# Attention and a gated FFN in one kernel: weights and first q/k by casting DMA, a new order of the first rows, masks as products on VectorE, FFN tiles of 368 and 208 tokens

## The chip, the cores and the metric

The kernel runs on one core of a Trainium2 chip. The time is the device time of one execution in microseconds (us), and the executions of one kernel spread by 0.6 to 2.2% in these runs (the four of the kernel before: 441.25 to 444.32 us). Each profile is of one execution. Its span is about 2 us shorter than the time reported for the run. TensorE (PE in the profile) does the matmuls, VectorE is DVE, ScalarE is ACT, GpSimd is POOL, and SyncE (SP) issues most DMAs. The granted clock is the share of the full clock that TensorE got, as the profile shows it. Results of matmuls stand in PSUM buffers, of which the program has a fixed number, until DVE or ACT has read them. Numbers like L330 are lines of the kernel that was profiled, so the same statement has different numbers in different kernels.

## The reference, cut to what matters

```python
def _attn_ref(q, k, v, beacon_k, beacon_v):     # q, k, v: (8, 8, 576, 64) f32, beacon: 16 keys
    k_all = np.concatenate([beacon_k, k], axis=2)
    v_all = np.concatenate([beacon_v, v], axis=2)
    scores = scale * np.matmul(q, k_all.transpose(0, 1, 3, 2))
    causal[:, Nb:] = np.triu(np.ones((S, S), dtype=bool), k=1)   # beacons are always visible
    scores = np.where(causal, -1000000000.0, scores)
    ...                                          # softmax
    return np.matmul(a, v_all)

def _moe_ref(x, w_gate, w_val, w_out):           # x: (4608, 512), d_ff = 1536
    gate = np.maximum(x @ w_gate, 0.0)
    val = x @ w_val
    return gate * val @ w_out                    # out: (4608, 512) f32

# x is the attention output with the 8 heads of a token side by side
```

There are 8 batches of 576 tokens. All matmuls run on bf16 operands, and all inputs are f32 in HBM, so every input must be cast on its way.

## The kernel before

Attention is done in 64 "bursts": one for each batch, pair of heads, and group of query rows. Group 0 is the first 368 rows, group 1 the last 208. A burst has two score tiles. ACT takes the exponentials of both, POOL zeroes the masked part of the result in place, TensorE multiplies by v (the AV matmuls), and DVE divides by the sum. When the four pairs of a batch are done, its rows of x are turned into xT and the FFN can use them.

```python
    def softmax(u, i):
        segs, cols = SLABS[u.g][i]
        p = psb.tile([P, 2, 512], BF16, name="p")
        A.activation(p[:, :, :cols], u.s[i][:, :, :cols], AF.Exp, scale=scale)
        for (kt, q0, n, c, mask) in segs:
            if mask:
                c, m, base = mask
                G.affine_select(out=p[:, :, c:c + m], in_=p[:, :, c:c + m], ...)   # POOL
        u.p.append(p)
```

Every load goes in f32 through one ring of 14 staging tiles, issued by SP, and is then cast by DVE, ACT or POOL (`cast(G)`). The output stores go through SP's queue too. `pump` refills the ring in one fixed order:

```python
        todo = (pq[0, 0] + [bk[0]] + pq[0, 1] + vl[0] + pq[0, 2] + pq[0, 3] + ch[0]
                + [bk[1]] + pq[1, 0] + ch[1] + pq[1, 1] + vl[1] + ch[2] + pq[1, 2] + pq[1, 3] + wol)
        def pump():
            while todo and Load.open < NSTG:
                todo.pop(0).issue()          # pq: q and k of a pair, vl: v, ch and wol: weights
```

In batches 0 and 1 the bursts go pair by pair, both row groups of a pair in turn, so that all 8 bursts of batch 0 are over before any FFN work. The FFN runs on nine tiles of 512 tokens, each with 12 pairs of gate and value matmuls (`up`) and 4 groups of output matmuls (`down`). A budget spreads it over the later bursts; one of these with its FFN work is a "tick":

```python
        def up(nf):                                       # 12 of these per tile
                for ki in range(KM): nc.tensor.matmul(g, wg[...], xT[:, ki, m0:m0 + 512], ...)
                A.activation(gs, g, AF.Relu)
                for ki in range(KM): nc.tensor.matmul(u, wv[...], xT[:, ki, m0:m0 + 512], ...)
                V.tensor_mul(st["h"][:, nf, :], gs, u)
        def down(ms):                                     # 4 of these per tile
                ...                                       # 12 matmuls of 512 columns
                A.copy(ob, o)
                nc.sync.dma_start(out[...], ob)
```

Of the kernel before, what the change touches and what calls it, by code (L numbers as in the profile page):

```python
# [22 lines left out]
def general_path(tc, q, k, v, beacon_k, beacon_v, out, ident, wg, wv, wo):  # L23
# [79 lines left out]
    with tc.tile_pool(name="gen_sb2", bufs=1) as sb, \  # L103
# [29 lines left out]
    ((((0, 0, 368, 0, (0, 112, 16)), (2, 240, 128, 368, (368, 128, 0))), 496),  # L133
     (((1, 112, 256, 0, (0, 128, 0)),), 256)),
    ((((0, 368, 208, 0, None), (1, 368, 208, 208, None), (4, 496, 80, 416, (416, 80, 0))), 496),
     (((2, 368, 208, 0, None), (3, 368, 208, 208, (208, 128, 0))), 416)),
# [6 lines left out]
def kernel(  # L143
# [24 lines left out]
    M_TILE = 512  # L168
    R = 2 * S // P
    scale = 1.0 / (D ** 0.5)  # L170
    assert (Nb, S, D, H) == (16, 576, 64, 8)

    const = ctx.enter_context(tc.tile_pool(name="const", bufs=1))
    ident = const.tile([P, P], BF16, name="ident")
    make_identity(nc, ident)
    ones = const.tile([P, 1], BF16, name="ones")
    nc.vector.memset(ones, 1.0)
# [5 lines left out]
    nc.vector.memset(rall, 1.0)  # L183
# [3 lines left out]
    qTs, kTs, vs = [], [], []  # L187
    for i in range(2):
        qTs.append(ring.tile([P, NP, S], BF16, name=f"qT{i}"))
        kT = ring.tile([P, NP, NKT * P], BF16, name=f"kT{i}")  # L190
        nc.gpsimd.memset(kT[:, :, Stot:], 0.0)
        kTs.append(kT)
        vx = ring.tile([P, NKT, H, D + 2], BF16, name=f"vx{i}")
        nc.gpsimd.memset(vx[:, :, :, D:], 1.0)
        vs.append(vx)

    NSTG = 14
    stage = main.enter_context(tc.tile_pool(name="stage", bufs=NSTG))
    c16 = main.enter_context(tc.tile_pool(name="c16", bufs=8))
# [3 lines left out]
    osb_p = main.enter_context(tc.tile_pool(name="osb", bufs=2))  # L203
# [3 lines left out]

    V, G, A = nc.vector, nc.gpsimd, nc.scalar
# [4 lines left out]
    class Load:  # L213
# [7 lines left out]
        def issue(self):  # L221
            Load.open += 1
            self.st = st = stage.tile([P, 576], FP32, name="stg")
            dma = nc.sync.dma_start
            heads = st[:, :H * D].rearrange("p (h d) -> p h d", d=D)
            if self.kind == "pair":
                src, b, p = self.key
                dma(st, src[b, 2 * p:2 * p + 2].rearrange("h (p r) d -> (h p) (r d)", r=R))
            elif self.kind == "beacon_k":
                dma(heads[:Nb], rows_of(beacon_k, self.key[0], 0, Nb))  # L230
            elif self.kind == "w":
                dst, src, ko, n0 = self.key
                dma(st[:, :512], src[ko * P:(ko + 1) * P, n0:n0 + 512])
            else:
                src, beacon, b, t = self.key
                s0 = t * P
                if beacon is not None:
                    s0 -= Nb
                self.n = n = min(P, S - s0)
                if s0 < 0:  # L240
                    dma(heads[:Nb], rows_of(beacon, b, 0, Nb))
                    dma(heads[Nb:], rows_of(src, b, 0, P - Nb))
                    self.n = P
                else:
                    dma(heads[:n], rows_of(src, b, s0, s0 + n))
            return self

        def cast(self, eng):
            Load.open -= 1
            cp = eng.copy if eng is A else eng.tensor_copy  # L250
            if self.kind == "w":
                dst, src, ko, n0 = self.key
                cp(dst[:, ko, n0:n0 + 512], self.st[:, :512])
            elif self.kind == "v":
                b, t, n = self.key[2], self.key[3], self.n
                cp(vs[b % 2][:n, t, :, 0:D], self.st[:n, :H * D].rearrange("p (h d) -> p h d", d=D))  # L256
            else:
                self.c = c = c16.tile([P, 576], BF16, name="c16")
                n, w = {"pair": (P, 576), "beacon_k": (Nb, 512)}.get(self.kind) or (self.n, 512)
                cp(c[:n, :w], self.st[:n, :w])  # L260
            return self

        def turn(self, cp):

            c = self.c
            if self.kind == "pair":
                src, b, p = self.key
                tp = f_ps.tile([P, R, D], BF16, name="f")
                for r in range(R):
                    for a in range(2):  # L270
                        rows = slice(a * D, (a + 1) * D)
                        nc.tensor.transpose(tp[rows, r], c[rows, r * D:(r + 1) * D], ident[rows, rows])  # L272
                dst = kTs[b % 2][:, p, Nb:Stot] if src is k else qTs[b % 2][:, p, :]
                cp(dst.rearrange("q (p r) -> q p r", r=R), tp.rearrange("q r p -> q p r"))  # L274
            elif self.kind == "beacon_k":
                tp = f_ps.tile([P, NP, Nb], BF16, name="f")
                for p in range(NP):
                    nc.tensor.transpose(tp[:, p], c[:Nb, p * P:(p + 1) * P], ident[:Nb, :Nb])
                cp(kTs[self.key[0] % 2][:, :, 0:Nb], tp)
            else:  # L280
                b, t, n = self.key[2], self.key[3], self.n
                dst = (kTs if self.kind == "k" else qTs)[b % 2]
                nc.sync.dma_start_transpose(dst[:, :, t * P:t * P + n], c[:n, :d_model])


# [3 lines left out]
    def qk(u):  # L289
        u.s, u.p = [], []  # L290
        for segs, cols in SLABS[u.g]:
            s = s_ps.tile([P, 2, 512], FP32, name="s")
            for (kt, q0, n, c, _) in segs:
                for a in range(2):
                    rows = slice(a * D, (a + 1) * D)
                    nc.tensor.matmul(s[:, a, c:c + n], kTs[u.b % 2][rows, u.pi, kt * P:(kt + 1) * P],  # L296
                                     qTs[u.b % 2][rows, u.pi, q0:q0 + n], start=True, stop=True)
            u.s.append(s)

    def softmax(u, i):  # L300
        segs, cols = SLABS[u.g][i]
        p = psb.tile([P, 2, 512], BF16, name="p")
        A.activation(p[:, :, :cols], u.s[i][:, :, :cols], AF.Exp, scale=scale)  # L303
        for (kt, q0, n, c, mask) in segs:
            if mask:
                c, m, base = mask
                G.affine_select(out=p[:, :, c:c + m], in_=p[:, :, c:c + m],  # L307
                                pattern=[[0, 2], [1, m]], compare_op=ALU.is_ge, fill=0.0,
                                base=base, channel_multiplier=-1)
        u.p.append(p)  # L310

    def av(u, opool):
# [3 lines left out]
        for p, (segs, cols) in zip(u.p, SLABS[u.g]):  # L316
            for (kt, q0, n, c, _) in segs:
                for j, qi in enumerate(qt):
                    r0, rn = QROWS[qi]
                    if q0 <= r0 and r0 + rn <= q0 + n:  # L320
                        blocks[j, kt] = (p, c + r0 - q0)
        first = True
        for j, qi in enumerate(qt):
            kts = sorted(kt for (jj, kt) in blocks if jj == j)
            m = 80 if qi == 4 else P
            for a in range(2):
                for kt in kts:
                    p, c = blocks[j, kt]
                    kr = P if kt < 4 else KT4
                    nc.tensor.matmul(o[:m, j, a, 0:D + 1], p[:kr, a, c:c + m],  # L330
                                     vs[u.b % 2][:kr, kt, 2 * u.pi + a, 0:D + 1],
                                     start=first, stop=(kt == kts[-1]), skip_group_check=True)
# [9 lines left out]
        if u.last:  # L342
            for qi in qt:
                r0, rn = QROWS[qi]
                dst = xT[:, :, u.b * S + r0:u.b * S + r0 + rn]
                if u.b:
                    nc.sync.dma_start_transpose(dst, u.x[:rn, qi, :])
                    continue
                tp = f_ps.tile([P, KM, P], BF16, name="f")
                for ki in range(KM):  # L350
                    nc.tensor.transpose(tp[:, ki, :rn], u.x[:rn, qi, ki * P:(ki + 1) * P], ident[:rn, :rn])
                (V.tensor_copy if qi % 2 else A.copy)(dst, tp[:, :, :rn])


    def ffn_tile(m):
        m0 = m * M_TILE
        st = {}

        def up(nf):
            def go():  # L360
                if nf == 0:
                    st["h"] = fsb.tile([P, NF, M_TILE], BF16, name="hT")
                g = f_ps.tile([P, M_TILE], FP32, name="f")
                for ki in range(KM):
                    nc.tensor.matmul(g, wg[:, ki, nf * P:(nf + 1) * P], xT[:, ki, m0:m0 + M_TILE],  # L365
                                     start=(ki == 0), stop=(ki == KM - 1))
                gs = fsb.tile([P, M_TILE], FP32, name="g")
                A.activation(gs, g, AF.Relu)  # L368
                u = f_ps.tile([P, M_TILE], FP32, name="f")
                for ki in range(KM):  # L370
                    nc.tensor.matmul(u, wv[:, ki, nf * P:(nf + 1) * P], xT[:, ki, m0:m0 + M_TILE],  # L371
                                     start=(ki == 0), stop=(ki == KM - 1))
# [235 lines left out]
```

## Time and profile before

| | before |
|---|---|
| time, median of 3 runs | 443.14 us (442.43 to 444.32) |
| span of the profile, mean granted clock | 438.5 us, 0.964 |
| TensorE busy | 377.0 us (86%) |
| DVE, ACT, POOL busy | 150.3, 193.2, 134.6 us |
| first FFN matmul | 36.0 us |

The next lines are from the page of the kernel before: busy time of each engine, then the span in 40 equal slices of 11 us (each digit is the busy share in tenths; PEclk is the granted TensorE clock), then the main DMA queue with its packets, its MB and its share of the 16 DMA engines' span.

```profile
span 438.5 us, 8104 instructions
PE 377.0 (86%) x3085; PEld 187.2 (43%) x3085; DVE 150.3 (34%) x349; ACT 193.2 (44%) x282; POOL 134.6 (31%) x295
...
PE   3668658784649979999999899999989989999995
...
PEclk9989988996859999999999999999999999999999
DMA  9954894798995278973984697559872012002002
...
q1 hardware_dynamic: 155936, 59.04, 62.4%
```

TensorE is nearly full from the thirteenth slice on (one slice shows 7). Before that it is partly idle throughout, with a hole in slices 10 to 12 (99 to 132 us) where the digits are 4, 6 and 4, while the DMA engines are at 8, 9 and 9 tenths and the clock falls to 6, 8 and 5. The table by windows of the kernel before measures the same in stretches. The columns are the window, its length, and for each engine its busy us and number of instructions (PE, weight loads, DVE, ACT, POOL), then the granted clock, the DMA share and GB/s.

```profile
0.00:24.00 24.00, 11.80 (x210) 8.55 (x210) 9.76 (x22) 10.44 (x13) 10.38 (x31) 1.00 1.00 273
24.00:60.00 36.00, 25.83 (x326) 15.20 (x326) 19.54 (x48) 16.32 (x24) 16.75 (x34) 0.95 0.67 204
60.00:90.00 30.00, 22.96 (x260) 12.39 (x261) 16.13 (x36) 12.76 (x18) 15.73 (x30) 0.89 0.74 182
90.00:135.00 45.00, 26.39 (x126) 10.49 (x125) 4.95 (x9) 9.57 (x16) 14.35 (x27) 0.77 0.98 181
135.00:170.00 35.00, 30.96 (x282) 15.60 (x281) 10.53 (x30) 18.20 (x26) 10.74 (x26) 1.00 0.48 109
```

From 90 to 135 us only 126 matmuls were issued, at a mean clock of 0.77. The waits of TensorE in the kernel before (who waited for whom, us in total, how often, longest) name the releasers:

```profile
PE f L272 <- DVE c L260: 16.4, 7, 4.7
PE o L330 <- POOL p L307: 13.7, 7, 9.8
PE s L296 <- ACT p L303: 9.6, 12, 1.2
PE f L365 <- ACT ob L383: 4.8, 1, 4.8
```

The first line, q and k that wait for their casts on DVE before TensorE can transpose them, is the longest in total, but all of it lies before 90 us. Two lines belong to the hole: AV (L330) waits for a POOL mask (L307), and an FFN group (L365) waits for the output copy on ACT (L383). To see why the mask was late, read POOL's own timeline in the kernel before (start us, duration, instruction, in brackets the idle time before it and what ended it):

```profile
117.86 0.61 POOL L256 CAST vx<-stg 128x512 bf16<-128x512 f32 x1 [4.33 <-DMA stg<-in_v_dram]
...
123.26 0.61 POOL L256 CAST vx<-stg 128x512 bf16<-128x512 f32 x1 [2.83 <-DMA stg<-in_v_dram]
124.44 0.61 POOL L260 CAST c<-stg 128x512 bf16<-128x512 f32 x1 [0.57 <-DMA stg<-in_k_dram]
125.52 0.61 POOL L260 CAST c<-stg 128x512 bf16<-128x512 f32 x1 [0.46 <-DMA stg<-in_q_dram]
126.08 1.10 POOL L307 TENSOR_SCALAR_AFFINE_SELECT p<-p 128x224 bf16<-128x224 bf16 x3
```

POOL took its instructions in the order of its program: the exponentials that ACT did before this mask had ended at 117.75 us, but the mask started at 126.08. It took 0.4 us a piece, and it stood behind casts that each waited for a load. TensorE's timeline shows the price in its first line (9.76 us), and the wait for the copy in its second:

```profile
108.03 1.87 PE L365 MATMUL f<-xT,wg 128*128 128x512 bf16 x4 [4.82 <-ACT ob L383]
...
126.52 0.35 PE L330 MATMUL o<-vx,p 128*128 128x65 bf16 x3 [9.76 <-POOL p L307]
```

The copy itself waited for its buffer, which a store in SP's queue had to free; that is ACT's timeline of the kernel before:

```profile
100.84 0.58 ACT L383 COPY ob<-f 128x512 f32<-128x512 f32 x1 [8.18 <-DMA out_dram<-ob]
107.40 0.58 ACT L383 COPY ob<-f 128x512 f32<-128x512 f32 x1 [5.97 <-DMA out_dram<-ob]
```

SP issued loads and transposes almost without a pause from 81 to 135 us, and the stores stood among them: the copy that ended at 90.06 us had its store issued at 98.33.

### The profile page before, as it was taken

How to read it: one execution, taken by the hardware profiler on the slowest of the kernel's cores; microseconds unless marked ns; L12 is line 12 of the kernel's file. 1: busy time of each engine (PE TensorE's matmuls, PEld its weight loads, DVE VectorE, ACT ScalarE, POOL GpSimd, SP SyncE). 2: the span in 40 equal slices, each digit the busy share in tenths (PEclk: the TensorE clock that was granted, in tenths of full speed). 3: DMA queues.
4: the chain of work that ended last, by engine and by line, in shares of the span. 5: the costliest groups of instructions: out<-in, count | busy, mean ns of one | idle time of the engine just before them, and what ended most of it. 6: DMA issues, size and time to landing. Idle time of an engine off the chain costs nothing. (4 is left out here: it accounts for less than half of the span.)

```text
span 438.5 us, 8104 instructions
## 1 busy us (share of the span) xinstructions
PE 377.0 (86%) x3085; PEld 187.2 (43%) x3085; DVE 150.3 (34%) x349; ACT 193.2 (44%) x282; POOL 134.6 (31%) x295
## 2 busy tenths in 40 slices
PE   3668658784649979999999899999989989999995
PEld 2454333431214434454444444454444445544442
DVE  3454564600114313441342144134314422430520
ACT  3453535411316545554554456455545554423321
POOL 3453442822345115333332243334323211000000
PEclk9989988996859999999999999999999999999999
DMA  9954894798995278973984697559872012002002
GB/s 201 334 186 130 234 358 126 151 168 175 199 192 99 40 164 178 148 139 97 209 147 103 158 191 128 139 144 180 142 170 51 0 48 85 19 3 96 0 16 87
DMA packets 155981, 59.62 MB, mean 136 GB/s; under 512 B 144672, under 2 KB 144672, under 8 KB 155936
## 3 DMA queue, kind: packets, MB, share of 16 engines
q1 hardware_dynamic: 155936, 59.04, 62.4%
q8 instruction: 26, 0.43, 0.4%
q14 instruction: 19, 0.16, 0.1%
HBM read 38.27 MB, written 9.44 MB: 109 GB/s over the span
## 5 line engine op out<-in xcount | busy, mean ns | idle before, releaser
L373 DVE TENSOR_TENSOR hT<-g,f 128x512 bf16<-128x512 f32 x108 | 74.3, 688 | 153.3 <-PE f L371 128.1
L307 POOL TENSOR_SCALAR_AFFINE_SELECT p<-p 128x256 bf16<-128x256 bf16 (+2 forms) x160 | 60.4, 390 | 207.8 <-ACT p L303 203.0
L303 ACT ACTIVATE p<-s 128x992 bf16<-128x992 f32 (+2 forms) x128 | 108.3, 864 | 35.5 <-PE s L296 33.5
L365 PE MATMUL f<-xT,wg 128*128 128x512 bf16 x432 | 114.8, 389 | 7.6 <-ACT ob L383 4.8
L371 PE MATMUL f<-xT,wv 128*128 128x512 bf16 x432 | 113.8, 387 | 0.2 <-ACT ob L383 0.2
L368 ACT ACTIVATE g<-f 128x512 f32<-128x512 f32 x108 | 64.5, 597 | 93.2 <-PE f L365 92.2
L380 PE MATMUL f<-wo,hT 128*128 128x512 bf16 x432 | 96.9, 379 | 0.0
L371 PEld LDWEIGHTS <-wv 128*128 128x128 bf16 x432 | 43.0, 100 | 53.8 <-issue 4.8
L365 PEld LDWEIGHTS <-wg 128*128 128x128 bf16 x432 | 40.2, 100 | 51.4 <-issue 11.6
L383 ACT COPY ob<-f 128x512 f32<-128x512 f32 x36 | 21.1, 585 | 92.8 <-PE f L380 54.5
L380 PEld LDWEIGHTS <-hT 128*128 128x128 bf16 x432 | 41.2, 98 | 47.1
L330 PE MATMUL o<-vx,p 128*128 128x65 bf16 (+2 forms) x888 | 43.8, 200 | 14.2 <-POOL p L307 13.7
L330 PEld LDWEIGHTS <-p 128*128 128x128 bf16 (+2 forms) x960 | 38.9, 109 | 27.4 <-POOL p L307 15.3
L338 DVE RECIPROCAL rall<-o 128x2 f32<-128x2 f32 (+2 forms) x88 | 15.4, 175 | 98.2 <-PE o L330 96.4
L296 PE MATMUL s<-qT,kT 64*128 64x208 bf16 (+4 forms) x512 | 39.0, 265 | 11.0 <-ACT p L303 9.6
L260 POOL CAST c<-stg 128x512 bf16<-128x512 f32 (+2 forms) x67 | 40.9, 622 | 8.5 <-DMA stg<-in_k_dram 4.9
L296 PEld LDWEIGHTS <-kT 64*128 64x128 bf16 x512 | 19.8, 98 | 38.6 <-issue 34.1
L339 DVE TENSOR_TENSOR x<-o,rall 128x128 bf16<-128x128 f32 (+2 forms) x88 | 34.0, 387 | 3.2
L256 POOL CAST vx<-stg 128x512 bf16<-128x512 f32 (+1 forms) x40 | 24.4, 616 | 25.0 <-DMA stg<-in_v_dram 25.0
L272 PE MATMUL f<-ident,c 64*64 64x64 bf16 x288 | 8.7, 220 | 20.6 <-DVE c L260 16.4
L272 PEld LDWEIGHTS <-c 64*64 64x64 bf16 x288 | 7.2, 132 | 23.5 <-DVE c L260 18.8
L274 ACT COPY qT<-f 128x576 bf16<-128x576 bf16 x5 | 3.2, 638 | 14.0 <-PE f L272 14.0
(35 smaller groups left out, 56.6 us busy)
## 6 DMA issues: line engine op xcount, KB each, us to landing
out_dram<-ob SPq DMA_DIRECT2D x36, 256.0 KB, 2.2
stg<-in_v_dram SPq DMA_DIRECT2D x24, 256.0 KB, 4.2
stg<-in_q_dram SPq DMA_DIRECT2D x24, 256.0 KB, 3.9
stg<-in_k_dram SPq DMA_DIRECT2D x18, 256.0 KB, 4.1
stg<-in_moe_w_gate_dram SPq DMA_DIRECT2D x12, 256.0 KB, 4.9
stg<-in_moe_w_val_dram SPq DMA_DIRECT2D x12, 256.0 KB, 5.0
stg<-in_moe_w_out_dram SPq DMA_DIRECT2D x12, 256.0 KB, 5.5
stg<-in_k_dram SPq DMA_DIRECT2D x8, 288.0 KB, 5.7
```

The source lines that it names most:

```text
L256: cp(vs[b % 2][:n, t, :, 0:D], self.st[:n, :H * D].rearrange("p (h d) -> p h d", d=D))
L260: cp(c[:n, :w], self.st[:n, :w])
L296: nc.tensor.matmul(s[:, a, c:c + n], kTs[u.b % 2][rows, u.pi, kt * P:(kt + 1) * P], qTs[u.b % 2][rows, u.pi, q0:q0 + n], start=True, stop= ...
L303: A.activation(p[:, :, :cols], u.s[i][:, :, :cols], AF.Exp, scale=scale)
L307: G.affine_select(out=p[:, :, c:c + m], in_=p[:, :, c:c + m], pattern=[[0, 2], [1, m]], compare_op=ALU.is_ge, fill=0.0, base=base, channel ...
L330: nc.tensor.matmul(o[:m, j, a, 0:D + 1], p[:kr, a, c:c + m], vs[u.b % 2][:kr, kt, 2 * u.pi + a, 0:D + 1], start=first, stop=(kt == kts[-1] ...
L339: V.tensor_mul(u.x[:m, i0:i0 + j1 - j0, u.pi * P:(u.pi + 1) * P].rearrange("p j (a d) -> p j a d", a=2), o[:m, j0:j1, :, 0:D], r.unsqueeze ...
L365: nc.tensor.matmul(g, wg[:, ki, nf * P:(nf + 1) * P], xT[:, ki, m0:m0 + M_TILE], start=(ki == 0), stop=(ki == KM - 1))
L368: A.activation(gs, g, AF.Relu)
L371: nc.tensor.matmul(u, wv[:, ki, nf * P:(nf + 1) * P], xT[:, ki, m0:m0 + M_TILE], start=(ki == 0), stop=(ki == KM - 1))
L373: V.tensor_mul(st["h"][:, nf, :], gs, u)
L380: nc.tensor.matmul(o, st["h"][:, nf, ms * P:(ms + 1) * P], wo[:, nf, :], start=(nf == 0), stop=(nf == NF - 1))
```

## The change

The intent is to fill TensorE earlier. (1) The weights, and q and k of batches 0 and 1 except for one pair's first rows, are loaded by GpSimd's DMAs, which write bf16 directly; their staging and casts fall away, and they are issued in the order in which they are used. (2) The mask becomes a product with a constant triangle on DVE; POOL keeps the casts of later batches. (3) In all batches the first 368 rows of all four pairs come first, so that the FFN can start after 4 bursts. (4) FFN tiles have 368 and 208 tokens, the row groups of a batch, instead of 512. (5) The order in DVE's, ACT's and TensorE's programs changes with it, and the output gets 3 buffers instead of 2. The diff, cut to its core (lines left out are marked by dots, and the comments are added here):

```diff
-    M_TILE = 512
+    tri = const.tile([P, 2, 240], BF16, name="tri")        # ones at and above the diagonal
-    NSTG = 14
+    NSTG = 6
-    osb_p = main.enter_context(tc.tile_pool(name="osb", bufs=2))
+    osb_p = main.enter_context(tc.tile_pool(name="osb", bufs=3))
...
-        for (kt, q0, n, c, mask) in segs:
-            if mask:
-                c, m, base = mask
-                G.affine_select(out=p[:, :, c:c + m], in_=p[:, :, c:c + m], ...)
+    def mask(u):
+        for i, (segs, cols, m) in enumerate(SLABS[u.g]):
+            p = u.p[i]
+            V.tensor_mul(p[:, :, :m], p[:, :, :m], tri[:, :, :m])
...
+    tiles = []
+    for b in range(B):
+        tiles += [(b * S, 368), (b * S + 368, 208)]
...
-            order = ([(p, g) for p in range(NP) for g in range(2)] if b < 2
-                     else [(p, g) for g in range(2) for p in range(NP)])
-            for p, g in order:
+            for p, g in [(p, g) for g in range(2) for p in range(NP)]:
...
+        def wload(dst, src, n0, n1):
+            G.dma_start(dst[:, :, n0:n1], src[:, n0:n1].rearrange("(j p) n -> p j n", p=P))
...
+        vl[0][0].issue()
+        vl[0][1].issue()
+        ...
+        direct(c0, 0, 1, 2, 0)              # casting DMAs: k, q of pair 1, first 368 rows
+        ...
+        direct(c0, 0, 2, NP, 0)             # pairs 2 and 3
+        vl[0][0].cast(G)
+        for n0, n1 in ((0, 256), (256, 512)):
+            wload(wg, moe_w_gate, n0, n1)
+            wload(wv, moe_w_val, n0, n1)
+        ...
+        direct(c0, 0, 0, NP, 1)             # the last 208 rows of all pairs
+        for n0, n1 in ((512, 1024), (1024, 1536)):
+            wload(wg, moe_w_gate, n0, n1)
+            wload(wv, moe_w_val, n0, n1)
...
+        burst(bursts[3])
+        ...
+        x_turn(bursts[3])                   # rows 0 to 367 of xT, by TensorE
+        next_ffn()
+        next_ffn()
+        ...
+        for p in range(NP):
+            burst(bursts[NP + p])
+            if p < NP - 1:
+                pair_turn(c0, 0, p + 1, 1, VA, (f_ps, f_ps))
+            next_ffn()
+            if p:
+                av(bursts[NP + p - 1], o_ps)
...
+        for j in range(0, NF, 4):
+            G.dma_start(wo[:, j:j + 4], moe_w_out[j * P:(j + 4) * P].rearrange("(j p) n -> p j n", p=P))
+        ...
+        direct(c1, 1, 0, 2, 2)              # q and k of batch 1
+        direct(c1, 1, 2, NP, 2)
```

## The prediction

> **What bounds the kernel now.** TensorE. The chain of waits that ended last is matmuls alone from 361 to 433 us; in the windows from 170 us on TensorE is busy 98-99% at full clock: the remaining 7 of 9 FFN tiles and 37 of 64 softmax bursts take 263 us against 261 us of bare matmuls. The time is lost before: until 170 us only 2 FFN tiles, 27 bursts and the transposes of two batches are done, about 102 us of matmuls (4 matmuls of 512 columns: 0.86 us; 18 AV matmuls: 0.73; a burst's scores: 0.45). So 68 us go to the ramp, 5 us to the tail. In the ramp the first FFN matmul comes at 36 us; between 90 and 135 us TensorE is busy about 26 of 45 us, at a clock down to 0.5. The waits show why: 9.8 us of AV for a POOL mask stuck behind POOL casts that wait for loads; 4.8 us for ACT's output copy, itself waiting up to 8.2 us for a store behind loads in one queue. The DMA share is 0.9-1.1 there.
>
> **What changes.** (1) Weights and q/k of batches 0 and 1 land as bf16: their casts (0.6-0.7 us each) and the staging waits go. The Trainium skill (DMA: Bandwidth & Descriptors, "SWDGE vs HWDGE vs iDMA") says only GpSimd-issued DMAs cast; before has none, so their rate is unmeasured here. (2) Masks leave POOL (62 us) for DVE: 128 products, scaled from DVE's 128x384 product (557 ns) with 16-bit operands at two per cycle, 0.25-0.4 us each, about 39 us. POOL no longer holds up AV. (3) Batch 0's first 368 rows of all pairs come first, so FFN needs 4 bursts (ACT-bound, 1.6 us each), not 8: first matmul near 17 us. (4) FFN tiles of 368 and 208 keep the columns but add 672 matmuls. The skill (TensorE: Matmul & The Clock Gate, "Back-to-back issue gap") gives N/2.4 + 2.5 ns; the trace agrees at 512 (216 ns). So +1.7 us. Relu rises from 64 to about 80 us, the hT product from 74 to about 102 us (0.15 us fixed, 288 instead of 108).
>
> **Sum (estimate).** Matmuls 367 us; lost before the first FFN 13; bursts 4-7 of batch 0, 3; waiting for weights or batch 1's q/k (behind all weights, about 14 MB, at 250-300 GB/s 47-56 us) 5; batch 1, 3; cold clock 3; tail 5; steady state 10: with 208 columns an up pair lasts 0.71 us on TensorE, and three PSUM buffers do not cover the two Exps (1.6-1.9 us) plus masks ahead of Relu and product: 0.6-1 us per tick, two ticks a batch. Span 406-409 us, reported 411 us. Nearly all of it is on the critical path, since TensorE idles in the ramp. Range 395 to 427. Chances: faster 0.94, same 0.05, slower 0.01.
>
> **What would show each step.** First FFN matmul at 14-20 us (timeline); no wait of AV for POOL, none over 4 us for an output copy; TensorE busy over 75% in the windows from 20 to 60 us, over 90% from 60 us on; DVE busy 200-220 us, POOL under 80. In steady state new short waits of FFN matmuls for Relu or hT products at 208 columns, some 10 us in total.
>
> **What would make it wrong.** Casting DMAs slower than plain ones or slowed by POOL's descriptor work (TensorE idles at 25-60 us, up to +20 us); 208-column matmuls held by weight loads (100 ns shown each against 87): up to +10 us; DVE as a new bottleneck; batch 2's loads colliding with late weights; or, the other way, no steady stalls: 395 us.

## The result

Ratios here are from the fast runs of both kernels in the same rounds on the same chip, so they are not quite the ratio of the medians.

| | before | after |
|---|---|---|
| time, median of 4 runs | 442.78 us (441.25 to 444.32) | 402.67 us (401.91 to 404.83) |
| ratio, 95% interval | | 0.9102 (0.9054 to 0.9150) |
| span of the profile, mean clock | 438.5 us, 0.964 | 400.7 us, 0.989 |
| first FFN matmul | 36.0 us | 24.0 us |

The change is worth 40 us, or 9%. The same parts of the page of the kernel after:

```profile
span 400.7 us, 9566 instructions
PE 369.3 (92%) x3745; PEld 237.9 (59%) x3745; DVE 192.0 (48%) x644; ACT 205.2 (51%) x372; POOL 68.5 (17%) x84
...
PE   2577979999799999999999999999999999999995
...
PEclk9999988999999999999999999999999999999998
DMA  8999997398599979877978794787769203101202
...
q1 hardware_dynamic: 149840, 45.37, 59.4%
q0 software_dynamic: 8784, 6.88, 11.3%
```

The hole is gone, and TensorE is at 0.9 from the seventh slice on, with one exception (0.7 at 100 to 110 us) before the last slice. The DMA digits are as high as before: the change did not relieve the DMA engines; TensorE waits less while they are busy. The windows of the kernel after say it in us:

```profile
0.00:24.00 24.00, 10.78 (x173) 6.97 (x174) 12.27 (x34) 10.41 (x15) 12.37 (x25) 1.00 1.04 152
24.00:60.00 36.00, 29.56 (x383) 19.45 (x384) 17.97 (x58) 17.65 (x33) 7.94 (x11) 0.96 1.11 185
60.00:90.00 30.00, 28.79 (x357) 17.98 (x356) 16.31 (x53) 17.82 (x30) 7.07 (x7) 0.93 0.69 140
90.00:135.00 45.00, 42.31 (x404) 27.06 (x404) 21.08 (x71) 22.64 (x43) 7.83 (x8) 1.00 0.93 157
135.00:170.00 35.00, 34.67 (x359) 23.14 (x356) 18.98 (x67) 20.32 (x38) 7.88 (x8) 1.00 0.91 164
```

Between 90 and 135 us the DMA share went from 0.98 to 0.93 only, but TensorE from 26.4 to 42.3 us busy, and its clock from 0.77 to 1.00. TensorE's waits of the kernel after have no line for a POOL mask and none for the output copy; what is left is short. Of the 16.4 us of waits for casts of q and k, only the wait for the first load is left (5.8 us); the transposes of later q and k (L307) wait 1.9 us in all:

```profile
PE f L304 <- ACT c L264: 5.8, 1, 5.8
PE f L394 <- ACT kq L310: 4.8, 6, 1.1
PE f L394 <- ACT g L391: 2.4, 7, 0.6
PE s L324 <- DVE kq L310: 2.4, 3, 0.8
PE f L388 <- DMA xT<-x: 2.4, 2, 2.2
```

The first is the arrival of the very first q and k. L394 <- L391 is the FFN waiting for a Relu: 2.4 us in all. TensorE's timeline of the kernel after gives the start of the FFN:

```profile
23.97 1.38 PE L388 MATMUL f<-xT,wg 128*128 128x368 bf16 x4 [0.61 <-DVE xT L380]
```

### Where the 40 us lie

Busy shares mislead a little, since a matmul that runs at half clock is busy too. So I count another way. I add up what the matmuls issued until time t would take back to back, and call t minus that sum the lost time. The costs per matmul are read from the trace: FFN matmuls of 512, 368 and 208 columns come every 216, 156 and 89 ns, AV matmuls every 31 to 36 ns, the score matmuls of a burst, two heads side by side, take 0.42 us (6 matmuls, first rows) or 0.50 us (10 matmuls, last rows), and transposes take 12 ns (q, k) or 58 ns (x). The sum is an estimate, good to a few us: the whole work is about 348 us in both kernels.

| lost time until (us) | 24 | 36 | 60 | 86 | 97 | 110 | 127 | 140 | 170 | 250 | 350 | 396 |
|---|---|---|---|---|---|---|---|---|---|---|---|---|
| before | 19 | 25 | 34 | 45.5 | 45.7 | 56 | 68 | 71 | 77 | 81 | 84 | 86 |
| after | 19 | 24 | 30 | 34 | 34 | 37 | 38 | 38 | 39.6 | 41.7 | 46.0 | 47.4 |

The columns are to be compared by their growth. Until 86 us the kernel after gains 11.5 us, and none of it in the first 24 us: the gain begins with FFN work in the gaps of bursts 4 to 7. From 97 to 140 us, the hole, it gains 21 us. From 140 to 170 us it gains another 4, and afterwards about 1. So over half of the gain is the hole. The table shows 38.6 of the 40 us, because the profiled run of the kernel before (440.26 us) was a little faster than the four that were compared.

### The profile page after: what moved, and what is told of

The parts are those of the page before. It is cut to its first block, busy times and chain, and to the rows that moved or that the text cites. A ratio compares the mean times of both kernels' runs of the same rounds, so it can differ in the third digit from the quotient of the medians.

```text
span 400.7 us, 9566 instructions
## 1 busy us (share of the span) xinstructions
PE 369.3 (92%) x3745; PEld 237.9 (59%) x3745; DVE 192.0 (48%) x644; ACT 205.2 (51%) x372; POOL 68.5 (17%) x84
## 3 DMA queue, kind: packets, MB, share of 16 engines
q0 software_dynamic: 8784, 6.88, 11.3%
## 4 chain that ended last, share of the span: by engine, by line
PE 77%; ACT 3%; SPq 2%; DMA 1%; issue 1%; DVE 1%; ACTq 0%; DVEq 0%
PE f L394 22%; PE f L410 21%; PE f L388 20%; PE o L357 8%; PE s L324 6%; DMA xT<-x 1%; ACT p L331 1%; ACT g L391 1%; SPq L375 1%; SPq L281 1%; ACT ob L413 1%; ACT kq L310 0%; PE f L307 0%; DVE hT L402 0%; SPq L244 0%
## 5 line engine op out<-in xcount | busy, mean ns | idle before, releaser
L402 DVE TENSOR_TENSOR hT<-g,f 128x208 bf16<-128x208 f32 (+14 forms) x288 | 93.1, 351 | 91.0 <-PE f L394 57.2
L394 PE MATMUL f<-xT,wv 128*128 128x368 bf16 (+1 forms) x768 | 127.1, 289 | 7.8 <-ACT kq L310 4.8
L388 PE MATMUL f<-xT,wg 128*128 128x368 bf16 (+1 forms) x768 | 127.1, 288 | 3.1 <-DMA xT<-x 2.4
L391 ACT ACTIVATE g<-f 128x368 f32<-128x368 f32 (+1 forms) x192 | 78.7, 413 | 88.3 <-PE f L388 46.2
L394 PEld LDWEIGHTS <-wv 128*128 128x128 bf16 x768 | 73.4, 99 | 33.9 <-issue 11.4
L388 PEld LDWEIGHTS <-wg 128*128 128x128 bf16 x768 | 69.5, 99 | 26.2 <-issue 5.3
L267 POOL CAST c<-stg 128x1024 bf16<-128x1024 f32 (+1 forms) x30 | 31.7, 1056 | 155.9 <-DMA stg<-in_q_dram 153.6
L337 DVE TENSOR_TENSOR p<-p,tri 128x256 bf16<-128x256 bf16 (+2 forms) x128 | 43.7, 364 | 12.6 <-ACT p L331 12.1
L324 PE MATMUL s<-kq 64*128 64x208 bf16 (+4 forms) x512 | 35.6, 260 | 3.2 <-DVE kq L310 2.4
L366 DVE TENSOR_TENSOR x<-o,rall 128x128 bf16<-128x128 f32 (+1 forms) x94 | 35.2, 375 | 3.4
L324 PEld LDWEIGHTS <-kq 64*128 64x128 bf16 x512 | 16.4, 96 | 21.8 <-issue 16.8
L307 PE MATMUL f<-ident,cs 64*64 64x64 bf16 x234 | 5.2, 212 | 2.0 <-DMA cs<-in_q_dram 0.9
L307 PEld LDWEIGHTS <-cs 64*64 64x64 bf16 x264 | 3.9, 124 | 4.4 <-issue 2.2
## 6 DMA issues: line engine op xcount, KB each, us to landing
wo<-in_moe_w_out_dram POOLq DMA_DIRECT2D x3, 512.0 KB, 15.2
```

The source lines that it names most:

```text
L267: cp(self.c[:n], self.st[:n])
L324: T.matmul(s[:, a, c:c + n], kq[rows, 0, u.pi, kt * P:(kt + 1) * P], kq[rows, 1, u.pi, Nb + q0:Nb + q0 + n], start=True, stop=True)
L337: V.tensor_mul(p[:, :, :m], p[:, :, :m], tri[:, :, :m])
L366: V.tensor_mul(u.x[:m, i0:i0 + j1 - j0, u.pi * P:(u.pi + 1) * P].rearrange("p j (a d) -> p j a d", a=2), o[:m, j0:j1, :, 0:D], r.unsqueeze ...
L388: T.matmul(g[:, :mn], wg[:, ki, nf * P:(nf + 1) * P], xT[:, ki, m0:m0 + mn], start=(ki == 0), stop=(ki == KM - 1))
L391: A.activation(gs[:, :mn], g[:, :mn], AF.Relu)
```

## The experiments

**Theory A**, that of the prediction: TensorE idled in the ramp because its own work stood behind DMAs in in-order queues, the masks behind POOL's casts and the output stores behind SP's loads. **Rival B**: what counts is when data land, so casting DMAs and the order of use bring the gain, and the mask hardly matters. **Rival C**: tiles that match the rows of a batch, and FFN work between bursts 4 and 7, fill the gaps, and the queues are secondary. Five kernels add parts of the change to the kernel before, and seven take parts out of the kernel after, or go on from it. All gave correct results. Ratios are to the kernel before in the same rounds; the kernel after has 0.9102, but from other rounds, so I do not trust a difference of under about 1% between it and another kernel.

| kernel | built from | us, median | ratio, 95% interval |
|---|---|---|---|
| b_masks | before, masks on DVE | 430.78 | 0.9659 (0.9591 to 0.9727) |
| b_store | before, stores from ACT | 453.07 | 1.0163 (1.0111 to 1.0215) |
| b_both | before, both | 431.49 | 0.9645 (0.9591 to 0.9698) |
| b_weights | before, weights by casting DMA | 427.04 | 0.9580 (0.9531 to 0.9629) |
| b_mw | before, masks and weights | 418.72 | 0.9445 (0.9406 to 0.9484) |
| a_poolmask | after, masks on POOL | 419.69 | 0.9446 (0.9407 to 0.9486) |
| a_late | after, no FFN before burst 7 | 409.17 | 0.9233 (0.9183 to 0.9283) |
| a_512 | after, FFN tiles of 512 | 415.47 | 0.9344 (0.9282 to 0.9405) |
| a_vlate | after, v behind q and k | 404.37 | 0.9109 (0.9063 to 0.9155) |
| a_turnV | after, PSUM copies on DVE | 402.04 | 0.9027 (0.8986 to 0.9067) |
| a_hyb | after, 512 from batch 3 on | 401.62 | 0.8950 (0.8880 to 0.9019) |
| a_best | after, a_hyb and a_turnV and a new start | 392.13 | 0.8821 (0.8775 to 0.8867) |

### b_masks: the masks alone, in the kernel before

```diff
-            if mask:
-                c, m, base = mask
-                G.affine_select(...)
...
+    def mask(u, i):
+        p = u.p[i]
+        for (kt, q0, n, c, m) in SLABS[u.g][i][0]:
+            if m:
+                c, m, base = m
+                t0 = P if base else 0
+                V.tensor_mul(p[:, :, c:c + m], p[:, :, c:c + m], tri[:, :, t0:t0 + m])
...
             if prev:
                 av(prev, o_ps)
+            if u:
+                mask(u, 0)
```

> The kernel before with only its masks moved from POOL to DVE as products with a stored triangle. Theory (in-order queues): in the kernel before, the 9.8 us wait of AV at 116-126 us is a mask that stands behind POOL casts of later loads; without it the hole closes, so 8-12 us less than before (about 431-435 us), no wait of AV for POOL. Rival (DMA bandwidth): batch 2's and 3's loads land no earlier, so TensorE only waits elsewhere: less than 3 us gained.

Measured: 3.4% faster, some 15 us by the ratio; the two profiles differ by less, 438.5 to 428.9 us of span. The 9.8 us wait of AV for POOL is gone, and the line of the window from 90 to 135 us, from the table by windows of b_masks, shows TensorE busy 35.81 us where it was 26.39:

```profile
90.00:135.00 45.00, 35.81 (x223) 15.85 (x224) 14.38 (x38) 15.49 (x24) 12.19 (x21) 0.89 1.00 181
```

The DMA share is 1.00. The output copy's wait stays: an FFN group waits 5.65 us for it. So moving the masks alone recovers at least what was expected, with the DMA engines as full as before. That speaks against rival B for this part.

### b_store: the output stores alone

```diff
-                nc.sync.dma_start(out[m0 + ms * P:m0 + (ms + 1) * P, :], ob)
+                A.dma_start(out[m0 + ms * P:m0 + (ms + 1) * P, :], ob)
```

> The kernel before with only its output stores issued from ACT's queue instead of the one queue that also issues all loads and transposes. Theory (in-order queues): the waits of ACT's output copy for its store (14.2 us in two waits, TensorE idle about 10 us between 97 and 111 us) vanish: 6-10 us less than before. Rival (DMA bandwidth): under 3 us, the wait reappears as a wait for batch 2's keys or queries.

Measured: 1.6% slower, which is under the 2% that a verdict of slower needs, so it is formally unclear; a gain of 6 to 10 us it is not, and my expectation failed. The wait for the copy did shrink: the FFN's 4.8 us are gone, and 2.6 us are left in another wait that is put down to a store. But TensorE's timeline of b_store shows where the time went:

```profile
130.88 0.34 PE L330 MATMUL o<-vx,p 128*128 128x65 bf16 x3 [16.77 <-POOL p L307]
```

AV waits 16.77 us for the same mask that cost 9.76 us before. TensorE came to it sooner (at 114.1 instead of 116.8 us), and the mask still stood behind the casts, whose loads landed no earlier: it started at 130.45 instead of 126.08 us. In the window from 90 to 135 us TensorE is busy even less, 24.53 us. The Trainium skill (DMA: Bandwidth & Descriptors, "Issuing engines are not separate DMA queues") says that DMAs issued from different engines end up on the same 16 DMA engines and interleave there. This run agrees: the store got another issuing queue, the DMA share from 90 to 135 us was 1.02 after 0.98, and the loads before the mask landed no sooner. At 127 us the lost time is 68 us in both kernels. So the wait that was removed stood in series with a later one, and the time went there. What b_store loses after that has in part another cause, which b_both shows.

### b_both: masks and stores together

The edit is the sum of the two diffs above.

> Both of the two edits above. Theory (in-order queues): the two gains add, 15-22 us less than before, about 421-428 us, and TensorE busy over 85% between 90 and 135 us. Rival (DMA bandwidth): less than 6 us.

Measured: 0.9645, the same as b_masks, over five runs; a sixth run was slow. The gain, 14 to 16 us, is at the lower edge of what was expected and no more than that of the masks alone. Yet the hole did close: TensorE is busy 41.22 of 45 us from 90 to 135 us (92%, over 85% was expected), after 35.81 in b_masks. It is ahead of b_masks by about 4 us of lost time at 170 us (63.9 against 68.5) and level with it at 350 us (75.1 in both). The waits of TensorE from 170 to 350 us show where that gain goes, in b_masks first, then in b_both:

```profile
PE s L302 <- ACT p L309: 3.2, 3, 1.2
PE s L302 <- ACT p L309: 7.5, 5, 2.0
```

The edit made ACT issue the stores. Each issue takes ACT about 0.35 us, between exponentials that TensorE waits for, and these waits grow by 4.3 us (b_store has 7.7 us there, the kernel before 3.2). So the store's half of theory A is real in the hole, some 4 us once the masks are out of the way, but this way of removing it costs as much later. No run has the stores on a queue that costs nothing, or only the third output buffer, so what the store's wait was worth in the change is not shown.

### b_weights: weights by casting DMA alone

```diff
-        todo = (... + ch[0] + [bk[1]] + pq[1, 0] + ch[1] + ... + ch[2] + ... + wol)
+        def wload(c):
+            for dst, src in ((wg, moe_w_gate), (wv, moe_w_val)):
+                G.dma_start(dst[:, :, c * 512:(c + 1) * 512], ...)
...
-                    if pieces and Load.open < NSTG and (early or s >= begin[pieces[0].key[2]] - 10):
+                    if pieces and Load.open < NSTG and s >= begin[pieces[0].key[2]] - 10:
```

> The kernel before with only the weights loaded by casting DMAs from POOL (3 gate/value chunks, 3 output chunks), without stage and casts; prefetch of batches 2 and up limited to 10 ticks ahead, which the freed stage makes needed. Theory (in-order queues): 36 loads leave the shared queue and 36 casts leave DVE and POOL, the prefetch of batch 2 starts before 70 us, and most of the hole of 97-135 us closes: 12-25 us less than before. Rival (the gain is the early FFN start and the masks): less than 8 us.

Measured: 4.2% faster, some 18 us. The longest wait of AV for a mask is 2.65 us, although the masks are still on POOL. The hole can thus be closed from either side: by taking the masks off POOL, or by taking weight loads and casts out of the queues, so that POOL does not stand and wait. Two things changed at once here, though. Without the weights the prefetch of batch 2 would have run far ahead, so I also limited it. How much of the 18 us belongs to the free queue, to the saved casts, or to the pacing, is open. Rival B holds in part: the weights alone bring no less than the masks alone.

### b_mw: both together

The edit is the sum of the diffs of b_masks and b_weights.

> The kernel before with masks on DVE and weights by casting DMA, both alone worth 15 and 19 us. If the two close the same hole (97-140 us), together they give about 20-25 us (about 419-424 us); if they close separate holes they add to about 34 us (410 us). What then still lies between this and the changed kernel (402 us) is the earlier FFN start, the order of rows and the tile sizes.

Measured: 5.6% faster, some 25 of the 40 us. The two alone add up to 3.4 + 4.2 = 7.6%, so they recover partly the same hole. The window from 90 to 135 us, from b_mw's table by windows:

```profile
90.00:135.00 45.00, 39.55 (x310) 18.87 (x309) 18.05 (x51) 22.17 (x33) 11.21 (x18) 1.00 0.81 164
```

TensorE has 39.55 of the 42.31 us that the kernel after has here, with the old burst order and 512-token tiles. Lost time at 170 us is 53 us, 13 more than in the kernel after, and 9 of these 13 us are there at 86 us already. So what is still missing comes mostly from the stages before: TensorE still waits 13.5 us for casts of q and k on DVE (16.4 in the kernel before, and in the kernel after 5.8 us for the first load alone), and its first FFN matmul comes at 38.9 us. The casting DMAs of q and k, the order of rows and the tiles were not tested one by one here.

### a_poolmask: the kernel after with its masks on POOL

```diff
-            V.tensor_mul(p[:, :, :m], p[:, :, :m], tri[:, :, :m])
+            for c, n, base in ((0, min(m, P), 0), (P, m - P, Nb)):
+                if n > 0:
+                    G.affine_select(out=p[:, :, c:c + n], in_=p[:, :, c:c + n], ...)
```

> The changed kernel with its masks back on POOL as selections, at the same place in the program. Theory (masks behind casts): in the changed kernel POOL waits 153 us for query loads; masks in that queue stand behind those waits, so AV waits for POOL again: 10-25 us more than the changed kernel. Rival (the loads come early enough once the weights are off the shared queue): within 3 us of the changed kernel.

Measured: 0.9446, so the masks on DVE are worth 3.4 points, about 15 us, in the kernel after too. TensorE's waits and then POOL's timeline in this run show that the larger part is at the start:

```profile
PE o L361 <- POOL p L339: 17.9, 3, 11.2
```

```profile
18.75 0.82 POOL L467 DMA_DIRECT2D wv<-in_moe_w_val_dram  x1
22.98 0.60 POOL L254 CAST vx<-stg 80x512 bf16<-80x512 f32 x1 [3.41 <-DMA stg<-in_v_dram]
23.55 3.19 POOL L339 TENSOR_SCALAR_AFFINE_SELECT p<-p 128x256 bf16<-128x256 bf16 x9
```

The first masks stand behind eight weight DMAs, each of which takes POOL 0.77 to 0.82 us to issue, two DMAs of k and q, and a cast that waits for its load. The first AV waits 11.16 us, and the first FFN matmul comes at 31.5 instead of 24.0 us. At 86 us the lost time is 46 instead of 34 us, 12 of the 15. In this kernel the casting DMAs and the product on DVE therefore belong together: POOL, which issues these DMAs, is a bad place for work that the critical path waits for.

### a_late: no FFN work between bursts 4 and 7

```diff
         x_turn(bursts[3])
-        next_ffn()
-        next_ffn()
...
                 pair_turn(c0, 0, p + 1, 1, VA, (f_ps, f_ps))
-            next_ffn()
             if p:
                 av(bursts[NP + p - 1], o_ps)
-        next_ffn()
         av(bursts[7], o_ps)
```

> The changed kernel with no FFN work before the last burst of batch 0 (the 7 FFN pairs that it puts among bursts 4-7 come after them). Theory (TensorE idles among these bursts): their 8.7 us of matmuls no longer fill idle time, so 5-9 us more than the changed kernel. Rival (weights or batch 1's q/k end the ramp anyway): within 2 us.

Measured: 0.9233, 1.3 points or about 6 us slower than the kernel after; the first FFN matmul comes at 39.6 us. This is as expected. Rival C's first half is real, but it is 6 of 40 us.

### a_512: tiles of 512 tokens from batch 2 on

```diff
-    for b in range(B):
-        tiles += [(b * S, 368), (b * S + 368, 208)]
+    tiles += [(0, 368), (368, 208), (S, 368), (S + 368, 80)]
+    tiles += [(i * HB, HB) for i in range(2, n_tokens // HB)]
```

> The changed kernel with tiles of 368, 208, 368, 80 tokens for batches 0 and 1 and 512 tokens from there on, so only the steady state differs. The prediction's term (three PSUM buffers do not cover Relu and product of 208-column tiles, 10 us): 8-11 us less than the changed kernel. Rival, from the trace of the changed kernel (single waits of 0.2-0.6 us, 1.4 us more fixed cost): 0-3 us less, or the same.

Measured: 0.9344, about 10 us slower, and neither theory had expected that. TensorE's waits in a_512:

```profile
PE s L324 <- DMA kq<-c: 8.4, 1, 8.4
PE f L388 <- DMA xT<-x: 5.6, 1, 5.6
```

Both come in the ramp, at 131 and 147 us. A 512-token tile that crosses a batch can only begin when rows of the next batch are done; the tile of tokens 1024 to 1535 needs 384 rows of batch 2, so both its row groups. My reading, which no further run tests, is that the FFN work therefore ran out earlier, and the bursts of the next batch reached keys that were not yet in place. Lost time goes from 35 us at 110 us to 57 us at 170 us. From 170 to 375 us, however, it grows by 2.8 us only, where the kernel after has grown from 39.6 to 46.2 us. So the small tiles do cost some 4 us in the steady state, and they pay for it in the ramp by being ready early.

### a_vlate: v of batch 0 behind the first q and k

```diff
-        vl[0][0].issue()
-        vl[0][1].issue()
...
+        first.cast(V, A)
+        vl[0][0].issue(V)
+        vl[0][1].issue(V)
         vl[0][0].cast(G)
...
-        first.cast(V, A)
```

> The changed kernel with the first two value loads of batch 0 issued only when the first keys and queries have landed (about 5.5 us instead of 3 us). In the changed kernel the keys and queries of pairs 2 and 3 land at 11.4 and 12.6 us, 8-9 us after issue, and the first FFN matmul comes at 24 us instead of the predicted 17. Theory (the start is bound by what the loads share): pairs 2 and 3 land 1-3 us earlier, first FFN at 21-23 us, 1-2.5 us less in all. Rival (the serial chain over ACT, DVE and TensorE sets the start): within 1 us.

Measured: 0.9109, the same. The q and k of pairs 2 and 3 landed about 2 us earlier, as intended, but then TensorE waited 2.43 us for a PSUM copy on DVE that stood behind the masks in program order. The first FFN matmul came at 22.87 us, 1.1 us earlier. Lost time is 32 instead of 34 us at 97 us, but the same 37 us at 110 us, since the FFN then waited 3.2 instead of 2.2 us for the xT of the next batch. So the start is held by a serial chain of loads, copies, exponentials, masks and divisions; the order of loads alone shortens it little, and a later wait takes that back.

### a_turnV: copies of q and k ahead of the masks, on DVE

```diff
-            burst(bursts[NP + p])
+            u = bursts[NP + p]
+            start(u)
+            qk(u)
+            softmax(u)
             if p < NP - 1:
-                pair_turn(c0, 0, p + 1, 1, VA, (f_ps, f_ps))
+                pair_turn(c0, 0, p + 1, 1, VV, (f_ps, f_ps))
+            mask(u)
...
-                pair_turn(c1, 1, u.pi + 1, 2, VA, (f_ps, f_ps))
+                pair_turn(c1, 1, u.pi + 1, 2, VV, (f_ps, f_ps))
```

> The changed kernel with the PSUM copies of the query transposes for bursts 4-7 and batch 1 on DVE instead of ACT, and ahead of the masks in DVE's queue. In the changed kernel FFN matmuls wait 4.8 us in six waits for these copies, which stand behind two Exps in ACT's queue and hold two of three PSUM buffers. Theory: 3-5 us less. Rival (DVE only takes over the delay, or the loads catch up): within 1 us.

Measured: 0.9027. The 4.8 us of waiting for ACT's copies are gone, and lost time at 97 us is 31 instead of 34 us. At 110 us it is 36.6 against 37.1: the FFN was then stopped by the transposed xT of the next batch, 3.0 us instead of 2.2. The ratio is better by 0.75 points, but from other rounds, and the lost times say 0 to 3 us. This is not settled.

### a_hyb: small tiles in the ramp, 512 tokens afterwards

```diff
-    for b in range(B):
+    for b in range(3):
         tiles += [(b * S, 368), (b * S + 368, 208)]
+    tiles += [(3 * S, 320)] + [(i * HB, HB) for i in range(4, n_tokens // HB)]
```

> The changed kernel with tiles of 368 and 208 tokens for batches 0-2, then one of 320 and five of 512. The run with 512 from batch 2 on lost 17 us between 110 and 150 us, where FFN work ran out while loads were awaited, but from 170 us on its lag grew by only 3 us against 7 us here. Theory (small tiles pay in the ramp because they are ready early and cost 4-5 us later): 3-5 us less than the changed kernel, no waits for batch 3's keys. Rival (readiness matters in every batch): the same or slower.

Measured: 0.8950, but with a wide scatter: one run took 395.1 us, and three of the six (402.74 to 403.73) count as slow only because they are over 1.5% above it, at nearly the same clock. The mean of all six is 400.9 us, which would be a ratio of about 0.901 to the 444.84 us of before; so the gain on the kernel after is 1 to 1.5 points. Lost time grows from 42.2 at 170 us to 45.3 at 375 us, 3.1 us against 6.6 in the kernel after. That fits the two readings of a_512: small tiles are good for the ramp and cost 3 to 4 us later. In the profiled run the net gain is small, since a_hyb had lost 2.6 us more than the kernel after by 170 us.

### a_best: what the experiments pointed to

```diff
+        def scores(u):
+            start(u)
+            qk(u)
+            softmax(u)                               # exponentials only
-        burst(bursts[0])
-        burst(bursts[1])
...
+        scores(bursts[0])
+        scores(bursts[1])
         pair_turn(c0, 0, 2, 0, VV, (f_ps, f_ps))
         pair_turn(c0, 0, 3, 0, VV, (f_ps, o_ps))
+        mask(bursts[0])
+        vl[0][1].cast(V)                             # was on ACT, between exponentials
+        mask(bursts[1])
...
-            if u.b:
+            if u.b > 1 or (u.b and not u.g):         # batch 1's last rows of xT by TensorE
                 nc.sync.dma_start_transpose(dst, u.x[:rn, qi, :])
```

To this come the edits of a_turnV and a_hyb.

> The changed kernel with four edits together: tiles of 512 from batch 3 on (alone 1.5% of the time before, by the ratios), PSUM copies of the query transposes on DVE ahead of the masks, the same order for the first four bursts (copies before masks, the value cast on DVE), and batch 1's last rows turned by TensorE after the FFN work of their tick instead of by DMA (a wait of 2-3 us at 104-108 us). If the terms add: 3-5 us from the tiles, 1-3 from the copies, 1-3 from the start, 1-3 from the transposes: ratio to the kernel before 0.875-0.89, first FFN at 20-22 us. If the ramp is bound by loads, the start's and copies' gains vanish in a later wait for batch 1's or 2's data and the ratio stays near 0.895.

Measured: 392.13 us (390.04 to 393.36, six runs), ratio 0.8821. This is faster than both kernels, about 3% under the kernel after, and inside the 0.875 to 0.89 expected if the terms add. It does not tell the four edits apart. The first FFN matmul comes at 21.35 us, and lost time is 17.4 us at 24, 27 at 97, 32.6 at 170 and 36 at 375 us. The largest waits of TensorE left in a_best are the arrival of the first load and copies of q and k:

```profile
PE f L304 <- ACT c L264: 5.7, 1, 5.7
PE s L324 <- DVE kq L310: 2.4, 3, 0.8
```

## Why the prediction was right, and where it was not

The direction and the size were right: 411 us predicted with 395 to 427, and 402.67 measured. That the total is so close is in part luck, since two errors of its terms pull against each other. Sums of the same kind, from the table of lost time:

| term | predicted | measured |
|---|---|---|
| all matmuls back to back | 367 | about 348 |
| lost before the first FFN matmul | 13 | 19 |
| ramp after that (bursts 4 to 7, weights and q/k, batch 1, cold clock) | 3 + 5 + 3 + 3 = 14 | 19, from 24 to 127 us |
| steady state | 10 | about 9, from 127 to 396 us |
| tail | 5 | about 5 |
| span | 406 to 409 | 400.7 |

- **AV no longer waits for POOL, and no output copy over 4 us: right.** Neither line is in the waits. The mask behind the casts is shown as a cause of the hole by b_masks (15 us by the ratio). The store behind the loads was a real wait of 4.8 us: b_store shows that its removal alone only moves the wait, b_both that it gains some 4 us in the hole once the masks are gone, and that issuing the stores from ACT takes as much back later.
- **TensorE over 75% busy from 20 to 60 us, over 90% afterwards: right.** It was 80% from 20 to 60, 96% from 60 to 90 (28.79 of 30) and 94% from 90 to 135.
- **First FFN matmul at 14 to 20 us: wrong, it came at 24.0 us.** The prediction took four bursts of exponentials of 1.6 us. The trace shows a chain: the exponentials run from 8.8 us to 20 us with gaps, among them a v cast of 1 us on ACT and copies on DVE behind masks, and after the last AV come reciprocal, product, transpose and copy, 3 to 4 us. a_vlate shows that earlier loads only move the wait; a_best, which reorders copies, masks and the cast, brings it to 21.35 us.
- **The sum of matmuls, 367 us: wrong by 19 us.** The prediction put 0.73 us on the AV of every burst. A group 1 burst has 18 AV matmuls and takes 0.64 us; a group 0 burst has 12 and takes 0.37 us. That is 14 us over 64 bursts (46.7 against 32.3); the rest I cannot assign, since the prediction does not itemise it. The same error made the steady state of the kernel before look perfect (263 us for 261); it was nearer 263 for 253. The 11 us too little in the two lost terms hide part of it, so the total is better than its parts.
- **Cost of small tiles: the size of the steady-state term was right, its content was not.** I expected waits for Relu and product of some 10 us. Waits for Relu were 2.4 us, none for the product is among the longer waits. Small tiles cost 3 to 4 us (a_512, a_hyb); the rest of the 9 us is not assigned.
- **More matmuls for +1.7 us, and weight loads as a risk: right, the risk did not occur.** The Trainium skill (TensorE: Matmul & The Clock Gate, "Back-to-back issue gap") gives N/2.4 + 2.5 ns for a matmul of N columns; four 208-column matmuls came in 0.355 us, 89 ns each, and four of 368 in 0.63 us, 156 ns each, as the formula says, although weight loads are shown at 99 ns each.
- **Work on DVE, ACT and POOL: close.** These are groups of the kernel after (instructions, busy us and mean ns, idle time before them):

```profile
L402 DVE TENSOR_TENSOR hT<-g,f 128x208 bf16<-128x208 f32 (+14 forms) x288 | 93.1, 351 | 91.0 <-PE f L394 57.2
...
L391 ACT ACTIVATE g<-f 128x368 f32<-128x368 f32 (+1 forms) x192 | 78.7, 413 | 88.3 <-PE f L388 46.2
...
L337 DVE TENSOR_TENSOR p<-p,tri 128x256 bf16<-128x256 bf16 (+2 forms) x128 | 43.7, 364 | 12.6 <-ACT p L331 12.1
```

  The hT product took 93.1 us (102 predicted), Relu 78.7 (80), the masks 43.7 (39). DVE was busy 192 us, just under the 200 to 220 predicted, and POOL 68.5 us (under 80). DVE did not become a bottleneck.
- **Casting DMAs slower than plain ones: hardly, at the same row length.** The 6.88 MB that they wrote came from 13.76 MB of f32 and took 11.3% of 16 engines' span of 400.7 us, 724 engine-us, so about 19 GB/s read for each engine. The plain queue before moved 13.5 GB/s, but most of its packets have only 256 bytes, so this is no comparison. The packet records allow a fairer one: casting packets that read 2,048 bytes of f32 took their data at 20.9 GB/s for each engine and those that read 2,304 bytes at 21.3; plain packets of these sizes in the kernel before, stores among them, moved 22.0 and 20.7. Shorter casting rows were slower, 16.1 GB/s at 1,024 bytes read.

What stays open: the split of b_weights' gain, the worth of a_turnV alone, what the store's wait was worth in the change, what the casting DMAs of q and k and the order of rows bring by themselves, and the 17 to 19 us that are lost in the first 24 us.

## What to carry to other kernels

When a wait names an engine whose own instruction is short, look at what stands in front of that instruction in the engine's program; here a 0.4 us mask cost 9.8 us because it stood behind casts that waited for loads. Two cures worked, neither of them a faster mask: another engine for the mask (b_masks), or fewer loads and casts in front of it (b_weights). Removing one wait of a chain may only move the time to the next wait, so test each alone and in combination, and look at what the cure itself costs: the stores issued by ACT gained some 4 us in the hole of b_both and lost as much to exponentials that came later. Size tiles for when their inputs are ready during the ramp, and for few instructions afterwards: small tiles for batches 0 to 2 and 512 tokens from then on gave the lowest ratio of the three arrangements tried here, though its runs scatter.

## What the Trainium skill lacked or had wrong

- TensorE: Matmul & The Clock Gate, "Back-to-back issue gap": it calls N/2.4 + 2.5 ns an isolated gap and gives 131 ns for sustained matmuls of 512 columns and 81 ns for 128. The chain of waits of the kernel after shows sustained streams of weight load and matmul at the formula instead (start us, us, what):

```profile
162.82 5.18 PE f L410 x24
...
365.72 10.36 PE f L410 x48
```

  That is 216 ns for each matmul of 512 columns, and 89 ns at 208 columns (0.355 us for four).
- DMA: Bandwidth & Descriptors, "SWDGE vs HWDGE vs iDMA": it says that only GpSimd's DMAs cast, but no page says what casting costs. Here POOL was held 0.73 to 0.82 us by each of the ten casting DMAs between 12.8 and 20.4 us, and DMAs that wrote 192 to 512 KB, twice that read, took medians of 5.3 to 15.2 us from issue to landing in the kernel after, while the DMA share was about 1.0 to 1.1. Plain loads of 256 KB took 4.1 to 4.8 us there, most of them later and under less load.
- No page gives a figure for what work on GpSimd loses behind such DMAs and casts, in the order of its program. In a_poolmask the first AV waited 11.16 us for it.
